# Window attention and PReLU FFN on one core: the turned slice order begins a pair later, y's last sums move behind the division, every second slice's PReLU goes through ScalarE

## The chip, the cores and the metric

The kernel runs on one core of a Trainium2 chip (8 cores). The metric is the device time of one execution in microseconds, the median of several runs.

## What is computed

Windowed attention over 8 batches, 8 heads, 576 positions and head size 64, and behind it a feed-forward layer over the 4608 tokens it gives:

```python
scores = scale * np.matmul(q, k.transpose(0, 1, 3, 2))
mask_plain = (rel >= 0) & (rel < 32)                        # heads 0 to 3
mask_dil = (rel >= 0) & (rel < 128) & (rel % 4 == 0)        # heads 4 to 7
scores = np.where(masks[None], scores, -1000000000.0)
attn = np.exp(scores - np.max(scores, axis=-1, keepdims=True))
attn = attn / (np.sum(attn, axis=-1, keepdims=True) + 1e-09)
x = np.matmul(attn, v).transpose(0, 2, 1, 3).reshape(4608, 512)
h = x @ w_in                                                # 512 to 2048
g = np.maximum(h, 0.0) + alpha * np.minimum(h, 0.0)
out = g @ w_out                                             # 2048 to 512
```

## The kernel before, in words

Each matrix product of the layer is made of three passes over float32r halves: every operand is split into a high half (a cast on ScalarE) and a low half (operand minus high half, on VectorE), and high x high, high x low and low x high are summed in PSUM. Attention is done for 32 pairs of heads, `Pair(b, c)`: `scores` (72 small matmuls), `maxima` (scale and mask from PSUM into `pr`, then the row maxima `nm`, on VectorE), `exponentials` (nine activations on ScalarE, with row sums), `divisions` and `turns` (VectorE: reciprocal, multiplication, transposition into `pt`), `values` (84 small matmuls), and `highs` and `lows`, which bring the result out of PSUM by ScalarE and VectorE.

The layer works on tiles of 512 tokens. Tiles 0 to 2 go slice by slice: a slice (t, f) is one tile and 128 of the 2048 hidden columns. `ffn_h` makes h of a slice (12 matmuls of 128x512 into one PSUM bank), `ffn_relu` and `ffn_sum` (relu(-h) on ScalarE, then one VectorE operation with `bal` = 1 - alpha) or instead `ffn_parts` (two VectorE operations, L490 and L491) apply the PReLU, `ffn_high` and `ffn_low` split g, and `ffn_y` (12 matmuls) adds the slice's share to four banks of y. Tiles 3 to 8 come afterwards, two at a time, in `paired_stage`, which multiplies block sums (Strassen's way) with weights from a ring of ten buffers filled by SP.

Every engine runs its instructions in the order of the program, which is written out by hand. The change lies in the loop `for n in range(CUT, NS)` with CUT = 6 and NS = 48, a step for each slice of the list `slices`: six of tile 0, sixteen of tile 1 (places 6 to 21), ten of tile 0 (22 to 31), sixteen of tile 2. Below, slice n or h(n), y(n), g(n) is the slice at place n of that list. Step n issues h of slice n + 1 and y of slice n - 1. From EARLY = 20 on it also works on a pair: even steps have the scores and maxima of a pair, the pair is divided and transposed two steps later, and its values come in the odd step three later. A step is `turned` when its y comes ahead of h; the other steps have h first. Up to step SECOND - 2 = 20, slices use `ffn_relu` and `ffn_sum`, and weights are still converted; from then on all slices use `ffn_parts`.

The four PSUM banks named "a" serve h, scores and values in turn, the banks "y" the sums of a tile. When a tile's sums are complete (slices 21 and 31, whose `ffn_y` stands in steps 22 and 32, and slice 47 behind the loop), `ffn_y` leaves a function in `ended`, which copies the four banks out and stores them. For tile 0 (slice 31) it adds the part sums that were stored before: `ffn_y` issues their loads into buffers of the tag "m" (five, shared with the PReLU's results), and L526 adds. `split_at` and `combine_at` name odd steps in which GpSimd sums weights for the paired stage (L568, L571) and ScalarE and VectorE split them (L576, L581). `late_ops` holds the token sums of the first paired tiles (`token_parts`: B11, B21, T1 and so on; casts at L666, subtractions at L663 and L669), given to certain steps by `plan_parts`.

Of the kernel before, what the change touches and what calls it, by code (L numbers as in the profile page):

```python
# [37 lines left out]
EARLY = 20  # L38
# [30 lines left out]
def tile_window_attention_prelu_ffn(  # L69
# [404 lines left out]
    def ffn_relu(t, f):  # L474

        ps = ms[t, f]
        m = ffp.tile([P, TT], F32, tag="m", name=f"m_{t}_{f}", bufs=5)
        nc.scalar.activation(out=m, in_=ps, func=AF.Relu, scale=-1.0)
        ms[t, f] = ps, m

    def ffn_sum(t, f):
        ps, m = ms[t, f]
        nc.vector.scalar_tensor_tensor(
            out=m, in0=m, scalar=bal[:, f:f + 1], in1=ps, op0=ALU.mult, op1=ALU.add)
        ms[t, f] = m

    def ffn_parts(t, f):
        ps = ms[t, f]
        m = ffp.tile([P, TT], F32, tag="m", name=f"m_{t}_{f}", bufs=5)
        nc.vector.tensor_scalar(out=m, in0=ps, scalar1=0.0, scalar2=al[:, f:f + 1], op0=ALU.min, op1=ALU.mult)  # L490
        nc.vector.scalar_tensor_tensor(out=m, in0=ps, scalar=0.0, in1=m, op0=ALU.max, op1=ALU.add)  # L491
        ms[t, f] = m

    def ffn_high(t, f):
        g = gbuf([P, 2, TT], F32R, f"g_{t}_{f}")
        nc.scalar.copy(out=g[:, 0, :], in_=ms[t, f])  # L496
        gs[t, f] = g
# [39 lines left out]
    ended = []  # L537
# [56 lines left out]
    for t in range(NSTD, NTILE, 2):  # L594
        for grp in range(NFP // GP):
# [17 lines left out]
            second = [wO[grp, c, j].rearrange("p f a n -> p (f a n)") for c in range(NC) for j in range(GP)]  # L613
# [5 lines left out]
    def slot(n):  # L619
        n %= NRING  # L620
        tag = ("w2_1", "w3_1", "xA1", "xA1", "g0")[n // 2]
        if tag not in ring:
            ring[tag] = (ffp if tag == "g0" else const).tile(
                [P, 8 if tag == "xA1" else 4, 2 * P], F32R, tag=tag, name=f"ring_{tag}",
                **({"bufs": 1} if tag == "g0" else {}))
        t = ring[tag].rearrange("p (s n) w -> p s (n w)", n=2)
        return t[:, n - 4 if tag == "xA1" else n % 2]

    def feed():
        if fed[0] < len(units):  # L630
            to, u = slot(fed[0]).bitcast(F32), units[fed[0]]
            nc.sync.dma_start(out=to if len(u.shape) == 2 else to.rearrange("p (c n) -> p c n", c=2), in_=u)
            fed[0] += 1
# [23 lines left out]
    def token_parts(t):  # L657


        k0, k1, z0, z1 = raw(t, 0), raw(t, 1), raw(t + 1, 0), raw(t + 1, 1)  # L660

        def diff(out, x, y):
            return lambda: nc.vector.tensor_tensor(out=out, in0=x, in1=y, op=ALU.subtract)  # L663

        def high(name, x):
            return lambda: nc.scalar.copy(out=part_of(name, 0), in_=x)  # L666

        def low(name, x):
            return lambda: nc.vector.tensor_tensor(  # L669
                out=part_of(name, 1), in0=x, in1=part_of(name, 0).bitcast(F32), op=ALU.subtract)  # L670

        zeroth = [high("B11", k0), low("B11", k0), high("B21", k1), low("B21", k1)]
        first = [diff(k0, z0, k0), high("T1", k0), low("T1", k0)]
        second = [
            diff(z0, z1, z0), high("T3", z0), diff(k0, z1, k0), high("T2", k0), low("T3", z0),
            diff(k1, k1, k0), low("T2", k0), high("B22", z1), high("T4", k1), low("B22", z1), low("T4", k1),
        ]
        return zeroth, first, second
# [488 lines left out]
    def early_sum(i):  # L1167


        place = []  # L1170

        def load():
            for q, tag in enumerate(("k", "q", "v", "pt")):
                x = att.tile([P, 4 * P], F32, tag=tag, name=f"wy{i}_{tag}").rearrange("p (a c n) -> p a c n", a=2, c=2)
                place.append(x)
                if i:
                    nc.sync.dma_start(out=x[:, 1], in_=wW[i, :, q % 2, q // 2])
                else:
                    high, low = (
                        weight(1, a, q // 2).bitcast(F32)[:, 2 * P * (q % 2):2 * P * (q % 2 + 1)].rearrange(  # L1180
                            "p (c n) -> p c n", c=2) for a in range(2))
                    nc.gpsimd.tensor_tensor(out=x[:, 1], in0=high, in1=low, op=ALU.add)
            combine_out(lambda q: place[q][:, 1])
            for x in place:
                split(x[:, 0], x[:, 1])

        def store():
            for q, x in enumerate(place):
                nc.sync.dma_start(
                    out=wY[i, q % 2, :, q // 2].rearrange("p a c n -> p (a c n)"), in_=x.rearrange("p a c n -> p (a c n)"))  # L1190

        return load, store
# [95 lines left out]
    late_ops = {}  # L1288

    def plan_parts():  # L1290
        zeroth, first, second = token_parts(NSTD)
        late_ops[NS - 9] = zeroth[:2]
        late_ops[NS - 5] = zeroth[2:] + first
        late_ops[NS - 3], late_ops[NS - 2], late_ops[NS - 1] = second[:5], second[5:8], second[8:]


    slices = [(0, f) for f in range(CUT)] + [(1, f) for f in range(NF)] + [(0, f) for f in range(CUT, NF)]
    slices += [(2, f) for f in range(HALF, NF)] + [(2, f) for f in range(HALF)]
    NS = len(slices)
# [127 lines left out]
    for k in range(GP):  # L1427
        first, last = early_sum(k)
# [6 lines left out]
    for n in range(CUT):  # L1435
        scored = pairs[NC + 1 + n] if n + 1 < NC else None
# [58 lines left out]
    score_at, value_at = {}, {}  # L1495
    for p in range(2 * NC, AHEAD):
        n = EARLY + 2 * (p - 2 * NC)
# [5 lines left out]
    for k in range(NFP):  # L1503
        n = SCRATCH + 1 + 2 * k + (2 if k > 1 else 0)
# [2 lines left out]

    for n in range(CUT, NS):
        scored, valued, divided = (at.get(n) for at in (score_at, value_at, divide_at))
        turned = n >= EARLY and n % 2 == 0  # L1510
        if turned:
            ffn_y(*slices[n - 1])
        if n + 1 < NS:
            ffn_h(*slices[n + 1])
        if n <= SECOND - 2:

            ffn_sum(*slices[n])
            ffn_high(*slices[n])
            for w in late:
                w.low()  # L1520
            words = [op for w in now for op in w.words()]
            for op in words[:1]:
                op()
            ffn_low(*slices[n])
            for op in words[1:]:
                op()
            if n + 1 <= SECOND - 2:
                ffn_relu(*slices[n + 1])
            late, now = now, [conversion() for _ in range(quota.pop(0) if quota else 0)]
            ahead()  # L1530
            for op in loads_early.get(n, ()):
                op()
            for w in late:
                w.high()
        elif late:
            late.pop().low()
        while turned and ended:
            ended.pop()()
        if divided:
            divided.divisions()  # L1540
            divided.turns()
        if scored:
            scored.scores()
        if SECOND - 2 <= n < NS - 1:
            ffn_parts(*slices[n + 1])
            ffn_high(*slices[n + 1])
            if not scored:
                ffn_low(*slices[n + 1])
        if not turned:
            ffn_y(*slices[n - 1])  # L1550
        if n in split_at:
            combined_high(split_at[n])
        if valued:
            valued.values()
        if scored:
            scored.maxima()
            ffn_low(*slices[n + 1])
            scored.exponentials()
        if valued:
            valued.highs()  # L1560
            valued.lows()
        while ended:
            ended.pop()()
        if n in split_at:
            combined_low(split_at[n])
        for u in pairs[2 * NC:AHEAD + 1]:
            if u is pairs[2 * NC]:
                due = 2 * (n == SECOND - 4,)
            else:
                due = scored is pairs[pairs.index(u) - 1], valued is pairs[pairs.index(u) - 1]  # L1570
            if due[0]:
                u.load_qk()
            if due[1]:
                u.load_v()
        if SCRATCH <= n < SCRATCH + NF:
            save(n - SCRATCH)
        for op in sums_early.get(n, ()):
            op()
        if n in combine_at:
            combine(combine_at[n], "xB1" if n < SCRATCH + 5 else "xA1")  # L1580
        if n == NS - 9:
            plan_parts()
        for op in late_ops.pop(n, ()):
            op()
        if n >= NS - NRING + 2:
            feed()

    ffn_y(*slices[-1])
    ended.pop()()
    feed()  # L1590
    feed()
    paired_stage()
# [74 lines left out]
```

## Time and profile before

| | |
|---|---|
| median of 3 runs | 853.82 us (852.75 to 858.84) |
| profiled execution | 856.63 us, span 854.8 us |
| TensorE busy | 828.4 us (97%) |
| VectorE, ScalarE, GpSimd busy | 634.6, 448.3, 126.3 us |
| granted TensorE clock, mean | 0.993 |

The span runs from the first to the last instruction; the profiled execution's own time is 1.8 us longer. TensorE's busy time counts matmuls whose ends are modelled, so neighbouring ones overlap by some 0.15 us in the rows: the distance between the starts of two rows tells more than their durations.

### The profile page before, as it was taken

The numbers are of one execution on the slowest core, as the hardware profiler recorded it, in microseconds if no ns is written. First come the engines' busy times: TensorE is split into PE (matmuls) and PEld (weight loads), VectorE is DVE, ScalarE is ACT, GpSimd is POOL, SyncE is SP. The second block draws the span as 40 slices with busy tenths as digits, with TensorE's granted clock in tenths as the row PEclk, the third lists the DMA queues.
The fourth block names the chain that finished last, engine by engine and source line by source line (L and its number), as shares of the span: only waits on it lengthen the run. The fifth ranks groups of instructions, "written<-read, shape, count | busy, mean of one in ns | idle before, by whom it ended". The sixth has DMA issues, their size and how long they took to land.

```text
span 854.8 us, 20630 instructions
## 1 busy us (share of the span) xinstructions
PE 828.4 (97%) x8167; PEld 670.1 (78%) x8167; DVE 634.6 (74%) x1073; ACT 448.3 (52%) x1268; POOL 126.3 (15%) x146
## 2 busy tenths in 40 slices
PE   7889999999989999999999999999999999999997
PEld 5677888788867877778778888788888888888886
DVE  4898888866857787688544988898469878843983
ACT  6786666434324434466534653666366436633650
POOL 0204253510313450030540000000000000000000
PEclk9999999999998999999999999999999999999999
DMA  7765567626897974577887668767766786667663
GB/s 241 257 206 176 188 220 264 204 97 211 269 302 239 304 241 135 180 246 236 260 276 239 194 192 280 249 190 213 223 176 183 219 266 194 195 192 195 193 216 132
DMA packets 123968, 185.71 MB, mean 217 GB/s; under 512 B 10464, under 2 KB 64352, under 8 KB 123872
## 3 DMA queue, kind: packets, MB, share of 16 engines
q1 hardware_dynamic: 123584, 184.13, 69.5%
q8 instruction: 65, 1.06, 0.6%
q14 instruction: 31, 0.25, 0.1%
q10 hardware_dynamic: 288, 0.26, 0.1%
HBM read 138.22 MB, written 46.14 MB: 216 GB/s over the span
## 4 chain that ended last, share of the span: by engine, by line
PE 78%; DVE 11%; DMA 4%; ACT 3%; issue 2%; SPq 1%; ACTq 0%; DVEq 0%
PE pA L684 14%; PE qA L1121 12%; PE h L470 10%; PE y L518 9%; PE pC L684 7%; PE qC L1121 6%; PE y L967 5%; PE pB L684 3%; PE qB L1121 3%; PE o L279 3%; PE s L254 2%; DVE w_dt.float32r L451 2%; DVE wa L440 1%; DMA wW<-wa 1%; DVE g L501 1%
## 5 line engine op out<-in xcount | busy, mean ns | idle before, releaser
L518 PE MATMUL y<-g,w_dt.float32r 128*128 128x512 f32 x576 | 142.4, 396 | 2.1 <-DVE g L501 1.1
L470 PE MATMUL h<-x,w_dt.float32r 128*128 128x512 f32 x576 | 141.0, 393 | 2.0 <-DVE w_dt.float32r L451 1.1
L518 PEld LDWEIGHTS y<-g,w_dt.float32r 128*128 128x128 f32 x576 | 107.9, 190 | 26.2 <-DVE g L501 1.9
L470 PEld LDWEIGHTS h<-x,w_dt.float32r 128*128 128x128 f32 x576 | 106.8, 188 | 25.7 <-DVE w_dt.float32r L451 1.6
L302 ACT ACTIVATE pr<-pr,nm 128x64 f32<-128x64 f32 x216 | 72.1, 336 | 27.2 <-DVE nm L292 27.2
L496 ACT CAST g<-m 128x512 fp32r<-128x512 f32 x48 | 29.6, 616 | 96.2 <-DVE m L491 92.4
L684 PE MATMUL pA<-parts_w,ring_w 128*128 128x512 f32 x234 | 58.4, 391 | 0.0
L684 PE MATMUL pA<-parts_w,ring_xA 128*128 128x512 f32 x228 | 56.4, 390 | 0.0
L837 DVE TENSOR_TENSOR gp<-stage,gp 128x512 fp32r<-128x512 f32 x80 | 53.5, 684 | 3.4 <-ACT gp L833 3.4
L833 ACT CAST gp<-stage 128x512 fp32r<-128x512 f32 x80 | 46.9, 618 | 9.3 <-DVE stage L830 8.1
L684 PEld LDWEIGHTS pA<-parts_w,ring_w 128*128 128x128 f32 x234 | 43.7, 188 | 9.6 <-ACT stage L726 0.5
L684 PEld LDWEIGHTS pA<-parts_w,ring_xA 128*128 128x128 f32 x228 | 42.6, 188 | 9.0 <-ACT stage L947 0.2
L501 DVE TENSOR_TENSOR g<-m,g 128x512 fp32r<-128x512 f32 x48 | 36.7, 764 | 16.6 <-ACT g L496 16.6
L1121 PE MATMUL qA<-gp,ring_xA 128*128 128x512 f32 x192 | 46.4, 390 | 0.0
L1121 PEld LDWEIGHTS qA<-gp,ring_xA 128*128 128x128 f32 x192 | 35.9, 188 | 7.5
L302 ACT ACTIVATION_READ_ACCUMULATOR pr<-pr,nm 128x1 f32 x216 | 40.7, 188 | 0.0
L1121 PE MATMUL qA<-gp,ring_w 128*128 128x512 f32 x168 | 40.5, 389 | 0.0
L1121 PEld LDWEIGHTS qA<-gp,ring_w 128*128 128x128 f32 x168 | 31.5, 188 | 6.5
L289 DVE SCALAR_TENSOR_TENSOR pr<-s,mask_sb 128x320 f32<-128x320 f32 (+1 forms) x48 | 21.6, 450 | 16.9 <-PE s L254 16.9
L811 DVE TENSOR_TENSOR stage<-pC,stage 128x512 f32<-128x512 f32 x25 | 17.2, 688 | 21.7 <-ACT stage L947 21.7
L279 PEld LDWEIGHTS o<-pt,v 32*64 32x64 f32 x1764 | 22.2, 134 | 14.1 <-issue 6.7
L490 DVE TENSOR_SCALAR m<-h,al 128x512 f32<-128x512 f32 x27 | 20.1, 743 | 16.4 <-PE h L470 15.9
(210 smaller groups left out, 1678.1 us busy)
## 6 DMA issues: line engine op xcount, KB each, us to landing
ring_w<-wS SPq DMA_DIRECT2D x68, 256.0 KB, 3.0
ring_xA<-wS SPq DMA_DIRECT2D x67, 256.0 KB, 3.2
v<-vX SPq DMA_DIRECT2D x24, 352.0 KB, 4.3
ring_g<-wS SPq DMA_DIRECT2D x33, 256.0 KB, 3.0
wO<-w_dt.float32r SPq DMA_DIRECT2D x32, 256.0 KB, 4.2
wS<-wc SPq DMA_DIRECT2D x16, 512.0 KB, 4.1
ring_w<-wO SPq DMA_DIRECT2D x32, 256.0 KB, 3.2
ring_xA<-wY SPq DMA_DIRECT2D x32, 256.0 KB, 3.1
```

The costliest lines, as they stand in the source:

```text
L279: nc.tensor.matmul(self.po[c][e * D:(e + 1) * D, a:z, :], lhsT=self.v[rows, (CUT0 + 1) * s + i, :], rhs=self.pt[rows, (r + a) * BK + (BQ i ...
L289: nc.vector.scalar_tensor_tensor(out=self.pr[:, a:z], in0=self.ps[i], scalar=SCALE, in1=mask_sb[:, self.mask + a:self.mask + z], op0=ALU.m ...
L302: nc.scalar.activation(out=self.pr[:, r, :], in_=self.ps[r // CUT0][:, r % CUT0, :] if self.onto else self.pr[:, r, :], func=AF.Exp, bias= ...
L470: nc.tensor.matmul(ms[t, f], lhsT=weight(0, a, f)[:, c * P:(c + 1) * P], rhs=half(t, c)[:, e, :], start=(c == 0 and n == 0), stop=(c == NC ...
L496: nc.scalar.copy(out=g[:, 0, :], in_=ms[t, f])
L501: nc.vector.tensor_tensor(out=g[:, 1, :], in0=ms.pop((t, f)), in1=g[:, 0, :].bitcast(F32), op=ALU.subtract)
L518: nc.tensor.matmul(ys[t][c], lhsT=weight(1, a, f)[:, c * P:(c + 1) * P], rhs=g[:, e, :], start=(first and n == 0), stop=(last and n == 2),)
L684: nc.tensor.matmul(to, lhsT=w[:, (2 * a + c) * P:(2 * a + c + 1) * P], rhs=part_of(name, e)[:, c * TT:(c + 1) * TT], start=start and c == ...
L833: nc.scalar.copy(out=self.pair(n)[:, 0], in_=self.whole(n))
L837: nc.vector.tensor_tensor(out=p[:, 1], in0=self.whole(n), in1=p[:, 0].bitcast(F32), op=ALU.subtract)
L967: nc.tensor.matmul(ys2[tt], lhsT=w[:, k * P:(k + 1) * P], rhs=g[:, e], start=j == 0 and n == 0, stop=j == GF - 1 and n == 2)
L1121: nc.tensor.matmul(named(to)[c], lhsT=w[:, b * P:(b + 1) * P], rhs=rhs[:, e], start=begins and k == 0, stop=i == GP - 1 and k == 2, skip_g ...
```

## The change

Five edits, all of them order or choice of engine; what is computed stays.

1. `turned` holds for even steps from 22 on; step 20 has h first.
2. `ended` in turned steps is emptied behind `divisions`, `turns` and `ffn_parts` (before: ahead of `divisions`). Only steps 22 and 32 have something in it.
3. In odd steps from 21 to 45, the PReLU of the even slice n + 1 (an odd one, counted from 1) goes by `ffn_relu` on ScalarE and `ffn_sum`; even steps keep `ffn_parts`.
4. A pair's `exponentials` move from the end of its even step into the next odd step, between `ffn_relu` and `ffn_sum`.
5. The token sums are given to other steps: `zeroth[2:]` (high and low of B21) from step 43 to 41, `second[9:]` (low of B22 and of T4) from step 47 to behind the last sums of the loop.

```diff
-        late_ops[NS - 9] = zeroth[:2]
-        late_ops[NS - 5] = zeroth[2:] + first
-        late_ops[NS - 3], late_ops[NS - 2], late_ops[NS - 1] = second[:5], second[5:8], second[8:]
+        late_ops[NS - 9], late_ops[NS - 7], late_ops[NS - 5] = zeroth[:2], zeroth[2:], first
+        late_ops[NS - 3], late_ops[NS - 2], late_ops[NS - 1], late_ops[NS] = second[:5], second[5:8], second[8:9], second[9:]
...
-        turned = n >= EARLY and n % 2 == 0
+        turned = n > EARLY and n % 2 == 0
...
-        while turned and ended:
-            ended.pop()()
         if divided:
             divided.divisions()
             divided.turns()
         if scored:
             scored.scores()
         if SECOND - 2 <= n < NS - 1:
-            ffn_parts(*slices[n + 1])
+            if n % 2:
+                ffn_relu(*slices[n + 1])
+                if n - 1 in score_at:
+                    score_at[n - 1].exponentials()
+                ffn_sum(*slices[n + 1])
+            else:
+                ffn_parts(*slices[n + 1])
+            while turned and ended:
+                ended.pop()()
             ffn_high(*slices[n + 1])
...
         if scored:
             scored.maxima()
             ffn_low(*slices[n + 1])
-            scored.exponentials()
...
     ffn_y(*slices[-1])
     ended.pop()()
+    for op in late_ops.pop(NS):
+        op()
```

## Rows read from the trace of the kernel before

**Rows 1.** The page's part 1: busy us, share of the span, instructions.
```profile
PE 828.4 (97%) x8167; PEld 670.1 (78%) x8167; DVE 634.6 (74%) x1073; ACT 448.3 (52%) x1268; POOL 126.3 (15%) x146
```

**Rows 2.** The chain that ended last, 150 to 190 us: start, us, what.
```profile
176.49 2.72 PE h L470 x12
179.20 0.90 PE s L254 x58
...
185.77 1.06 PE o L279 x56
```

**Rows 3.** Timeline of TensorE, 150 to 190 us: start, us, what, idle before.
```profile
157.06 3.49 PE L518 MATMUL y<-g,w_dt.float32r 128*128 128x512 f32 x13
161.69 2.79 PE L518 MATMUL y<-g,w_dt.float32r 128*128 128x512 f32 x11 [1.14 <-DVE g L501]
164.32 2.88 PE L470 MATMUL h<-x,w_dt.float32r 128*128 128x512 f32 x12
```

**Rows 4.** Timeline of VectorE, 148 to 192 us.
```profile
160.95 0.68 DVE L501 TENSOR_TENSOR g<-m,g 128x512 fp32r<-128x512 f32 x1
```

**Rows 5.** Timeline of TensorE, 236 to 300 us.
```profile
249.32 2.88 PE L518 MATMUL y<-g,w_dt.float32r 128*128 128x512 f32 x12
254.51 0.30 PE L279 MATMUL o<-pt,v 32*64 32x32 f32 x4 [2.31 <-DVE pr L289]
...
257.81 1.46 PE L279 MATMUL o<-pt,v 32*64 32x32 f32 x78 [2.14 <-DVE m L491]
...
263.57 2.90 PE L470 MATMUL h<-x,w_dt.float32r 128*128 128x512 f32 x12
...
274.03 3.02 PE L518 MATMUL y<-g,w_dt.float32r 128*128 128x512 f32 x12
...
287.31 3.02 PE L518 MATMUL y<-g,w_dt.float32r 128*128 128x512 f32 x12
```

**Rows 6.** Busy time by windows of 2 us; PEclk is the granted clock.
```profile
260.00:262.00 2.00, 2.00 (x6) 1.52 (x6) 1.93 (x4) 0.00 (x0) 0.94 (x1) 0.50 0.74 242
```

**Rows 7.** Timeline of VectorE, 225 to 266 us.
```profile
247.18 0.69 DVE L526 TENSOR_TENSOR ob<-y,ob 128x512 f32<-128x512 f32 x1 [6.65 <-DMA ob<-part]
248.74 2.03 DVE L526 TENSOR_TENSOR ob<-y,ob 128x512 f32<-128x512 f32 x3 [0.87 <-DMA ob<-part]
...
251.93 0.78 DVE L317 STREAM_TRANSPOSE pt<-pr 128x576 f32<-128x576 f32 x1
...
257.06 0.69 DVE L491 SCALAR_TENSOR_TENSOR m<-h,m 128x512 f32<-128x512 f32 x1
```

**Rows 8.** Timeline of TensorE, 300 to 400 us.
```profile
339.86 1.05 PE L279 MATMUL o<-pt,v 32*64 32x32 f32 x78 [1.27 <-DVE m L491]
...
354.74 0.86 PE L254 MATMUL s<-k,q 64*32 64x64 f32 x64 [0.75 <-DVE ob L528]
```

**Rows 9.** Timeline of VectorE, 305 to 372 us.
```profile
339.12 0.69 DVE L491 SCALAR_TENSOR_TENSOR m<-h,m 128x512 f32<-128x512 f32 x1
...
354.00 1.28 DVE L528 COPY ob<-y 128x512 f32<-128x512 f32 x2
```

**Rows 10.** Timeline of ScalarE, 270 to 306 us.
```profile
273.16 1.05 ACT L576 CAST wc<-wsum_xA 128x1024 fp32r<-128x1024 f32 x1 [0.55 <-PE y L518]
```

**Rows 11.** Groups by line, 163 to 357 us: busy us, mean ns, idle before.
```profile
L302 ACT ACTIVATE pr<-pr,nm 128x64 f32<-128x64 f32 x108 | 36.1, 335 | 4.1 <-DVE nm L292 4.1
L490 DVE TENSOR_SCALAR m<-h,al 128x512 f32<-128x512 f32 x27 | 20.1, 743 | 16.4 <-PE h L470 15.9
...
L669 DVE TENSOR_TENSOR parts_w<-raw_xB,parts_w 128x1024 fp32r<-128x1024 f32 x7 | 8.4, 1221 | 1.1 <-ACT parts_w L666 1.1
L666 ACT CAST parts_w<-raw_xB 128x1024 fp32r<-128x1024 f32 x7 | 7.4, 1058 | 5.0 <-DVE raw_xB L663 4.9
```

**Rows 12.** Line L478, the relu: ns min/median/max, first and last start, forms.
```profile
L478 ACT ACTIVATE m<-h x21: 586/598/681, 39.6 to 159.9; 128x512 f32<-128x512 f32 x21
```

**Rows 13.** Line L311, the multiplication in the division, in the same columns.
```profile
L311 DVE TENSOR_TENSOR pr<-pr,rs x24: 757/760/1678, 177.6 to 636.3; 128x576 f32<-128x576 f32 x24
```

## The prediction

> **What bounds the kernel now.** I read the page first: TensorE is busy 828.4 of 854.8 us [rows 1], so some 26 us of idle time are all that can be won, and only the loop over steps n = 20 to 47 (156 to 356 us) is touched. There I took the idle times out of TensorE's timeline; y(n), h(n) are the products of slice n, counted from 0. In undisturbed steps two slices need 13.28 us, from the start of one y at 274.03 to that two steps on at 287.31 [rows 5], with no idle time noted: they are TensorE's own work, which no shuffling on VectorE or ScalarE shortens. Twelve of its matmuls need 2.72 us, a pair's scores 0.90, its values 1.06 [rows 2]. Four places lose time.
> First, step 20: y(18) begins at 157.06, so h(21), two blocks later, could begin at 157.06 + 2 x 2.72 = 162.50; it begins at 164.32 [rows 3]: 1.8 us lost, because y(19) stands ahead of it and waits for the low half of g(19), written from 160.95 for 0.68 us [rows 4].
> Second, steps 32 to 34: y(32) begins at 249.32 and ends 2.72 later, at 252.04. The values of step 33 (1.06) and y(33) (2.72) should be through at 255.9, but h(35) begins at 263.57 [rows 5]: 7.6 us lost. Some 5 us of it is idle time (2.31 and 2.14 in the rows, and 0.55 between them); the rest is the clock, granted at 0.50 (1.2 GHz) from 260 to 262 after this idle time [rows 6].
> Third, step 45: the values wait 1.27 us for VectorE's L491. Fourth, the first scores of the paired stage wait 0.75 us for a copy of ob [rows 8].
>
> **The change, part by part.**
> *Turned order from n > 20.* At step 20, h(21) and the scores now come ahead of y(19). h(21) begins at 157.06 + 2.72 = 159.8 and ends at 162.5, the scores end at 163.4; g(19) is complete at 161.64 [rows 4]. Nothing waits: the whole 1.8 us is won. Behind h(21) its evacuation is queued on VectorE, which still works on the slice before; it has until y(21), due at 171.6, which covers it. If h(21) itself were to wait for w_in(15), whose low half is converted just before that time, up to 1 us would go back.
>
> *Final sums behind division and parts (steps 22 and 32).* At step 32 VectorE stands 6.65 us at the first of the four adds (L526), waiting for the DMA that brings back the partial sums, and again for the second; the four are through at 250.77 [rows 7]. Only then come division, transposition (from 251.93 for 0.78), parts(33) (0.74 + 0.69), the maxima of the scores (1.7), low(33) (0.68) and parts(34), whose L491 ends at 257.75 [rows 7]. The values of step 33 need the four PSUM banks that h(33), two score tiles and h(34) hold, so they start at 257.81 [rows 5]. In the new order division, transposition and parts(33) run inside the 6.65 us of waiting: h(33) was through before 245.7 (249.32 less 2.72 for h(34) and 0.90 for the scores), so parts(33) end near 247.1, as the first transfer lands. The adds keep their time, to 250.77, since their loads are issued from the same place of SP's queue. Then maxima to 252.5, low(33) to 253.2, and the sum for slice 34 (one operation of 0.7 us in place of two) to 253.9. The values begin at 253.9 in place of 257.81: 3.9 us won. As only 1.8 us stay idle (252.1 to 253.9), little more than the 1.14 at step 20, behind which eleven matmuls took 161.69 to 164.32 [rows 3], which is full speed, I take the slow stretch as gone too: 7.6 - 1.8, less 0.1 for the restart, gives 5.7 us. Bounds: 3.9 if the clock falls all the same, 7.6 if the partial sums land earlier. The stores of the sums stay directly behind their adds, so what SP issues behind them keeps its place; it is needed a step later and lies covered.
> At step 22 two copies of y's banks (0.7 each) move behind parts(23). h(23) is then through at 177.1, 1.9 earlier than now, parts to 178.5, copies to 179.9. y(22) uses the same banks and is due at 180.7: covered by 0.8 us; if that cover fails, TensorE loses what is missing, 0 to 1.4 us.
>
> *Relu on ScalarE in odd steps.* It replaces thirteen VectorE operations of 0.74 us [rows 11] by a relu of 0.60 us [rows 12] on ScalarE, which is busy 52% [rows 1]. The Trainium skill, page ScalarE: Activation LUTs, section Rules for kernel authors, tells authors to put relu, max and min on VectorE and not on ScalarE. This case's rows show the opposite order for a 128x512 f32 tile out of PSUM, 0.60 against 0.74 us, so the measurement decides; by the rule each relu would be the dearer of the two, and the sum would stay as it is, since ScalarE has the time.
> The exponentials move with it: in twelve odd steps they now stand behind the relu and ahead of the slice's high half. Nine of them take 9 x 0.335 = 3.0 us [rows 11]. In time from the start T of an odd step's h: relu 2.9 to 3.5, exponentials to 6.5, high to 7.1. Now the high part of the combined weights begins at 273.16 [rows 10] in step 35, whose T is 274.03 less 2.85 + 2.72 + 1.06, so at T + 5.8; it would begin 1.3 us later. So the values' copies, the weights' low part, division and transposition also come some 1.2 us later and end near T + 12.5. Parts of the next slice can't begin before T + 12.4 anyway, when its h is through. Then maxima, low and the one-operation sum end at T + 17.4; the next values are due at T + 18.95. The delay is hidden by 1.5 us, and nothing is paid in most steps. The multiplication in the division takes 0.76 us alone and up to 1.68 in other places [rows 13], namely beside GpSimd's weight sums; the 12.5 contains 1.6.
>
> *Token sums spread otherwise.* One cast (1.05) and one subtraction (1.22) [rows 11] move from step 43 to 41; low B22 and low T4 (1.22 each) go behind the last copies. Steps 39 and 41 now have such a pair between the delayed weights and the division: there the sum ends at T + 19.1 to T + 19.3 against 18.95. I charge 0.2 and 0.3 us; bounds 0 and 1.2 each. In step 43 VectorE's relief of 1.2 us and the exponentials' delay cancel, but slice 46 needs one operation on VectorE in place of two, so the values of step 45 wait about 0.5 us where they waited 1.27 for an L491 begun at 339.12 [rows 8, 9]: 0.8 us won, bounds 0 and 1.3. At the end the copies of ob no longer stand behind three subtractions, which held them to 354.00 [rows 9]; low T2 alone is ahead, so they end before the scores come: 0.7 won. B22 and T4 are first multiplied six products of 1.36 us on, which covers their low halves.
>
> Sum: 1.8 + 5.7 + 0.8 + 0.7 = 9.0 won, 0.5 paid: 8.5 us. The profiled execution took 856.63 us with its span of 854.8; it would be 848.1. It lies 2.8 us above the median of 853.82. I take the sum off the median, since none of these waits hangs on one execution: 845.3 us, 1.0% less. The paired stage behind is the same work and keeps what is won.
>
> **The rivals.**
> *The values of step 33 wait for another thing.* The relu of slice 34 writes a buffer that the first finished sum leaves, so it waits for that tile's store, issued after 247.9; before, the first operation on that buffer came only after 256. If the store takes over 4.5 us, the relu is late for the sum, and each us more is one lost; with more idle time the clock may fall again. For it: the loads issued for step 32 kept VectorE waiting 6.65 us [rows 7]. Against: the store starts when those loads are through. Cost 2 to 4 us: 847.3 to 849.3.
> *All of it goes.* The partial sums land earlier, and the remaining 1.8 us and the 0.5 each of steps 39, 41 and 45 vanish: 842.5.
> *Slower: the odd steps no longer close.* Relu, exponentials and high on ScalarE and the chain on VectorE up to the next values form a ring around each pair of steps, with a slack of 1.5 us by the rows. If the later division meets more of GpSimd's sums (0.9 us on the multiplication, as much on the small addition ahead of it), every us beyond the slack is paid in each of eleven pairs of steps. From 0.8 us beyond it on, the gain of 8.5 is a loss; 1.6 beyond gives 845 + 18 = 863. For it: steps 39 and 41 already have no slack. Against: the 12.5 above contains the long multiplication. Beside this stands the Trainium skill, page SBUF — State Buffer, section Who interferes with whom: a VectorE instruction with two SBUF inputs and a reading GpSimd contend, and the later one is blocked entirely. The trace agrees in kind (0.76 against 1.68).
> *It does little.* The waits come back a step on, because TensorE arrives earlier at the next late operand: 849.5 to 854.
>
> **How the numbers follow.** Forecast 845.3 us, 843.3 to 847.3: 0.55. Store: 0.17. All gone: 0.10. Little: 0.12. Slower ring: 0.06. From 842 to 850 lies 0.84 of this; the upper end takes in the store rival and the bound of 3.9 for the clock. A measurement of this kernel can tell about 1% from no change, which is 8.5 us, and the forecast stands on this edge: faster by over 1% takes a little over half of the first case and the third, 0.44; within 1% 0.51; slower 0.05.
>
> **What would show it.** Right: in the trace after, h(21) directly behind y(18) with no idle time near step 20; division and transposition before the adds of ob at step 32, one idle time of about 1.8 us ahead of the values of step 33 and a granted clock of 1.00 behind it; a wait of 0.5 us or less at step 45 and none of the first scores of the paired stage; two steps still 13.28 us. Wrong: idle times ahead of the values in many odd steps, h of even steps waiting for banks that the values held, or a clock of 0.50 after step 33.

## The result, and the profile after

The changed kernel takes 846.06 us (median of 4 runs, 843.14 to 847.11) against 855.24 of before beside it: a ratio of 0.9884, 95% interval 0.9837 to 0.9931. Run again later with more runs it gave 847.0 against 855.05 us, 0.991 (0.9891 to 0.9928). So some 8 us are won, 0.9 to 1.2%. The profiled execution's span fell from 854.8 to 845.0 us. The page of after, part 1:

```profile
PE 827.2 (98%) x8167; PEld 668.7 (79%) x8167; DVE 629.0 (74%) x1060; ACT 453.4 (54%) x1281; POOL 128.2 (15%) x146
```

TensorE's own work is the same in count [rows 1]; ScalarE has thirteen instructions more and VectorE thirteen fewer, the relus. What went is nearly all idle time: TensorE's busy time fell by 1.2 of the 9.8 us. TensorE's timeline of after, from step 20 on (start, us, what, idle before and its releaser), answers to [rows 3]:

```profile
155.58 2.88 PE L518 MATMUL y<-g,w_dt.float32r 128*128 128x512 f32 x12
158.87 3.29 PE L470 MATMUL h<-x,w_dt.float32r 128*128 128x512 f32 x12 [0.41 <-ACT w_dt.float32r L448]
162.09 0.97 PE L254 MATMUL s<-k,q 64*32 64x64 f32 x72
162.99 3.06 PE L518 MATMUL y<-g,w_dt.float32r 128*128 128x512 f32 x12
165.89 2.88 PE L470 MATMUL h<-x,w_dt.float32r 128*128 128x512 f32 x12
...
247.28 3.00 PE L518 MATMUL y<-g,w_dt.float32r 128*128 128x512 f32 x12
250.21 0.56 PE L279 MATMUL o<-pt,v 32*64 32x32 f32 x6
252.19 1.17 PE L279 MATMUL o<-pt,v 32*64 32x32 f32 x78 [1.41 <-DVE m L483]
253.28 4.36 PE L518 MATMUL y<-g,w_dt.float32r 128*128 128x512 f32 x12
257.48 2.88 PE L470 MATMUL h<-x,w_dt.float32r 128*128 128x512 f32 x12
...
333.02 1.05 PE L279 MATMUL o<-pt,v 32*64 32x32 f32 x78 [0.35 <-DVE m L483]
334.00 3.02 PE L518 MATMUL y<-g,w_dt.float32r 128*128 128x512 f32 x12
...
345.38 1.52 PE L684 MATMUL pA<-parts_w,ring_w 128*128 128x512 f32 x6
346.83 0.97 PE L254 MATMUL s<-k,q 64*32 64x64 f32 x72
347.73 1.67 PE L684 MATMUL pC<-parts_w,ring_w 128*128 128x512 f32 x6
```

h(21) stands directly behind y(18), with a wait for the weight of that slice (L448); the values of step 33 still wait, and the y behind them takes 4.36 us in place of the 2.9 to 3.0 of other y; the waits of step 45 and of the first scores of the paired stage are 0.35 us and nothing [rows 8]. The windows of after say why y(33) is long: the granted clock (last but two) is at 0.50, 1.2 GHz.

```profile
250.00:252.00 2.00, 0.77 (x8) 0.38 (x6) 1.97 (x5) 1.82 (x11) 0.00 (x0) 1.00 1.13 328
252.00:254.00 2.00, 1.81 (x80) 1.66 (x81) 0.32 (x2) 2.00 (x10) 0.00 (x0) 0.70 0.90 292
254.00:256.00 2.00, 2.00 (x6) 1.53 (x5) 2.00 (x5) 1.07 (x3) 0.00 (x0) 0.50 1.12 354
```

VectorE around step 32 of after shows the new order, and what it still waits for ([rows 7] show before):

```profile
240.55 0.78 DVE L317 STREAM_TRANSPOSE pt<-pr 128x576 f32<-128x576 f32 x1
243.60 0.75 DVE L490 TENSOR_SCALAR m<-h,al 128x512 f32<-128x512 f32 x1 [2.27 <-PE h L470]
244.38 0.69 DVE L491 SCALAR_TENSOR_TENSOR m<-h,m 128x512 f32<-128x512 f32 x1
246.48 2.69 DVE L526 TENSOR_TENSOR ob<-y,ob 128x512 f32<-128x512 f32 x4 [1.41 <-DMA ob<-part]
...
250.79 0.68 DVE L501 TENSOR_TENSOR g<-m,g 128x512 fp32r<-128x512 f32 x1
251.39 0.74 DVE L483 SCALAR_TENSOR_TENSOR m<-m,bal,h 128x512 f32<-128x512 f32 x1
```

Transposition and parts(33) (L490, L491) lie ahead of the adds (L526); the idle time at them fell from 6.65 to 1.41 us. Lengths between marks of TensorE's timeline show where the 9.8 us of the two profiled executions are, and serve for all kernels below (us; each is the difference of two starts, the last one from pC to the end of the span):

| kernel | y(18) to h(22) | y(32) to h(35) | wait at step 45 | pA to pC | pC to end | time, ratio to before |
|---|---|---|---|---|---|---|
| before | 10.97 | 14.25 | 1.27 | 3.31 | 499.3 | |
| after | 10.31 | 10.20 | 0.35 | 2.35 | 497.3 | 846.06, 0.9884 |
| after, again | 10.30 | 10.27 | 0.35 | 2.35 | 497.3 | 847.0, 0.991 |
| turned order alone | 10.05 | 14.24 | 1.27 | 3.31 | 497.5 | 853.8, 0.9981 |
| last sums alone | 13.47 | 10.51 | 1.27 | 3.30 | 497.5 | 849.95, 0.9937 |
| relu and exponentials alone | 10.76 | 13.34 | 1.59 | 3.26 | 497.4 | 856.6, 1.0013 |
| token sums alone | 13.52 | 14.37 | 0.17 | 2.36 | 497.1 | 852.99, 0.9964 |
| order without relu | 9.84 | 10.32 | none | 2.36 | 497.3 | 846.92, 0.9905 |
| loads early | 9.74 | 7.24 | 0.35 | 2.35 | 497.2 | 842.64, 0.9864 |
| loads early, sums between | 10.99 | 7.48 | 0.36 | 2.35 | 497.2 | 845.09, 0.9884 |
| relu, exponentials as before | 10.98 | 13.60 | none | 2.35 | 497.0 | 856.62, 1.0012 |
| order and early loads, no relu | 9.97 | 7.81 | 0.15 | 2.35 | 496.9 | 844.32, 0.9864 |

Two differences of the first two lines are not the change's. The stage ahead of step 20, which no edit touches, ended 1.5 us earlier in the execution of after (y(18) at 155.58 against 157.06), and from pC to the end before took 499.3 us where all eleven others take 496.9 to 497.5: its trace has 1.79 us in which TensorE waits for nothing that the profile shows, and no other trace has them. The row, from before:

```profile
440.94 0.85 PE L967 MATMUL y<-gp,ring_w 128*128 128x512 f32 x3 [1.79 <-issue]
```

### The profile page after: what moved, and what is told of

It reads as the page before. It is cut to its first block, busy times and chain, and to the rows that moved or that the text cites. A ratio compares the mean times of both kernels' runs of the same rounds, so it can differ in the third digit from the quotient of the medians.

```text
span 845.0 us, 20627 instructions
## 1 busy us (share of the span) xinstructions
PE 827.2 (98%) x8167; PEld 668.7 (79%) x8167; DVE 629.0 (74%) x1060; ACT 453.4 (54%) x1281; POOL 128.2 (15%) x146
## 4 chain that ended last, share of the span: by engine, by line
PE 74%; DVE 12%; ACT 6%; DMA 5%; issue 2%; SPq 1%; ACTq 0%; DVEq 0%
PE pA L684 14%; PE qA L1121 12%; PE h L470 8%; PE y L518 7%; PE pC L684 7%; PE qC L1121 6%; PE y L967 5%; PE pB L684 3%; PE qB L1121 3%; PE s L254 2%; PE o L279 2%; DMA ws<-w_in 2%; DVE w_dt.float32r L451 2%; ACT pr L302 2%; DVE wa L440 1%
## 5 line engine op out<-in xcount | busy, mean ns | idle before, releaser
L478 ACT ACTIVATE m<-h 128x512 f32<-128x512 f32 x34 | 20.4, 599 | 27.9 <-PE h L470 22.4
L451 DVE TENSOR_TENSOR w_dt.float32r<-wa,w_dt.float32r 128x512 fp32r<-128x512 f32 x26 | 21.5, 841 | 10.6 <-ACT w_dt.float32r L448 10.4
```

What stands on the lines that cost most here:

```text
L451: nc.vector.tensor_tensor(out=self.dst[1], in0=self.a.bitcast(F32), in1=self.dst[0].bitcast(F32), op=ALU.subtract)
```

## The experiments

**Each edit alone.** Four kernels, each the kernel before with one part of the change.

The turned order:

```diff
-        turned = n >= EARLY and n % 2 == 0
+        turned = n > EARLY and n % 2 == 0
```

> The kernel before with the turned order from step 22 on, nothing else. Theory (each wait of TensorE ends by its own edit): h(21) directly behind y(18), the wait at step 20 gone or shrunk to a short wait for w_in(15); the block up to h(22) 1.5 to 2.1 us shorter, steps 32, 45 and the paired stage as before, in all about 852. Rival (the gain of step 20 only came from an earlier arrival in that one execution): h(22) no earlier, no change.

0.9981 (0.9962 to 1.0), so about 1.6 us, as expected, though the interval reaches down to no change. The block is 10.05 us long. How much it wins depends on the execution: the four traces with the old order there took 10.76 to 13.52 us for this block (12.2 on average), the eight with the turned order 9.74 to 10.99 (10.3). In two of the four, those of the last sums and of the token sums, y(19) waited twice and its matmuls then ran slowly, at a granted clock of about half; in the eight the clock stayed at 1.00 there. From the last sums' kernel, with the window behind the waits:

```profile
155.09 2.88 PE L518 MATMUL y<-g,w_dt.float32r 128*128 128x512 f32 x12
158.91 0.50 PE L518 MATMUL y<-g,w_dt.float32r 128*128 128x512 f32 x1 [0.93 <-ACT g L496]
160.68 4.31 PE L518 MATMUL y<-g,w_dt.float32r 128*128 128x512 f32 x11 [1.27 <-DVE g L501]
```
```profile
162.00:164.00 2.00, 2.00 (x6) 1.52 (x6) 1.26 (x2) 0.53 (x1) 0.00 (x0) 0.51 0.57 195
```

The two turned kernels with 10.98 and 10.99 us show what then comes late: the scores behind h(21) waited 0.90 us for the load of q.

The last sums:

```diff
-        while turned and ended:
-            ended.pop()()
         if divided:
...
             ffn_parts(*slices[n + 1])
+            while turned and ended:
+                ended.pop()()
```

> The kernel before with the last sums behind division, transposition and parts, nothing else. Theory: division, transposition and parts(33) leave the chain behind the adds, two operations for slice 34 stay on it; the values of step 33 begin 3.1 us earlier against y(32), some 5.3 us behind its start; y(33) still at the clock of 0.50; 3 us won in all, about 851. Rival (the relu did it): values as late as before, 8.5 us behind the start of y(32).

0.9937 (0.9913 to 0.996), 5.4 us, more than expected, while its trace shows 3.7 us less for the block at step 32 and the clock again at half. The values begin 5.12 us behind y(32), where 5.3 were expected: the mechanism holds without the relu. That leaves 1.7 us between the median and this block; the interval allows 3.4 to 7.4. The profiled execution, 852.04 us, was itself 2.1 us above the median of 849.95, and the slow y(19) at step 20 made its block there 2.5 us longer than in the trace of before. Whether the other executions were spared that is not shown.

The relu on ScalarE with the late exponentials (edits 3 and 4, as in the diff of the change):

> The kernel before with relu on ScalarE in odd steps and the exponentials behind it, nothing else. Theory: steady pairs of steps stay at 13.3 us; at step 33 one operation of 0.7 less, so 0.7 us won; at step 45 the late exponentials push the token sums and the values wait as long as before or 0.4 longer; in all within 1 us of the kernel before. Rival (ScalarE relieves VectorE everywhere and most of the gain is here): 3 us or more won, waits at step 45 gone.

1.0013 (0.999 to 1.0036): nothing won. The block at step 32 is 0.9 us shorter, but step 45 waits 1.59 us where before waited 1.27, and behind this wait the clock falls (0.61, then 0.53) and y(45) takes 4.59 us. So its trace gives back at step 45 what it won at step 32. TensorE and the windows of this kernel:

```profile
337.43 1.05 PE L279 MATMUL o<-pt,v 32*64 32x32 f32 x78 [1.59 <-DVE m L483]
338.41 4.59 PE L518 MATMUL y<-g,w_dt.float32r 128*128 128x512 f32 x12
```
```profile
336.00:338.00 2.00, 0.57 (x55) 0.57 (x59) 1.35 (x2) 1.08 (x2) 0.00 (x0) 1.00 0.00 0
338.00:340.00 2.00, 2.00 (x48) 1.68 (x38) 1.94 (x7) 0.78 (x7) 0.00 (x0) 0.61 0.28 52
340.00:342.00 2.00, 2.00 (x7) 1.59 (x6) 2.00 (x3) 1.27 (x2) 0.00 (x0) 0.53 0.71 215
```

The token sums:

```diff
-        late_ops[NS - 9] = zeroth[:2]
-        late_ops[NS - 5] = zeroth[2:] + first
-        late_ops[NS - 3], late_ops[NS - 2], late_ops[NS - 1] = second[:5], second[5:8], second[8:]
+        late_ops[NS - 9], late_ops[NS - 7], late_ops[NS - 5] = zeroth[:2], zeroth[2:], first
+        late_ops[NS - 3], late_ops[NS - 2], late_ops[NS - 1], late_ops[NS] = second[:5], second[5:8], second[8:9], second[9:]
```

> The kernel before with the token sums spread as after, nothing else. Theory: the wait of the values at step 45 falls from 1.27 to 0.2 or less, as VectorE gets to that division 1.2 us earlier, and the first scores of the paired stage do not wait; 2 us won, about 852. Rival (step 45 was won by the relu): its wait stays at 1.2, only 0.9 won at the end.

0.9964 (0.994 to 0.9989), 3.1 us; its own marks show 1.1 at step 45 and 0.95 from pA to pC. The wait of step 45 is 0.17 us, less than in the changed kernel: this edit won it, not the relu.

```profile
340.97 1.05 PE L279 MATMUL o<-pt,v 32*64 32x32 f32 x78 [0.17 <-DVE m L491]
```

The four ratios together give 1.6 + 5.4 + 3.1 less 1.1, that is 9.0 us, within the error of the whole.

**The changed kernel again, and without its relu.**

> The changed kernel once more, for a narrower interval and a second trace. Theory (single edits add up: 1.6 + 5.4 + 3.1 less 1.1): 846 to 848, ratio near 0.990; from pC of the paired stage to the end 497.3 us as in all four single edits, so that the 1.8 us wait inside that stage in the trace of before was that execution's alone; clock 0.50 for a stretch behind step 33 again. Rival (the change also shortens the paired stage): 495 us or less from pC to the end.

As expected: its five lengths repeat those of after to 0.1 us, the clock falls behind step 33 again, and pC to the end is 497.3.

The second kernel has the turned order, the last sums and the token sums, with `ffn_parts` for all slices and the exponentials at the end of the even step:

```diff
-            if n % 2:
-                ffn_relu(*slices[n + 1])
-                if n - 1 in score_at:
-                    score_at[n - 1].exponentials()
-                ffn_sum(*slices[n + 1])
-            else:
-                ffn_parts(*slices[n + 1])
+            ffn_parts(*slices[n + 1])
...
             ffn_low(*slices[n + 1])
+            scored.exponentials()
```

> The three edits of order without the relu and the late exponentials: turned order, last sums and token sums as after, odd steps with two VectorE operations and the exponentials where they were. Theory (relu and late exponentials win nothing beside the others): within 1 us of the changed kernel, 845 to 848; values of step 45 wait 0.2, block y(32) to h(35) 10.5. Rival (they need each other): 2 us or more slower than the changed kernel.

846.92 against 847.0 us on the same chip: relu and late exponentials win nothing that can be told beside the other three edits (the intervals are some 2 us either way). Its block at step 32 takes 10.32 us against 10.27.

**What is left of the stall.** SP issues the stores of a weight slice (`save` of step 31) ahead of the loads of the part sums. Here they go behind (`REST` is 31, the place of the slice whose sums end there):

```diff
         if turned:
             ffn_y(*slices[n - 1])
+        if n == REST + 1:
+            save(REST - SCRATCH)
...
-        if SCRATCH <= n < SCRATCH + NF:
+        if SCRATCH <= n < SCRATCH + NF and n != REST:
             save(n - SCRATCH)
```

> The changed kernel, with the stores of one weight slice (step 31) issued behind the loads of the part sums instead of ahead of them. Theory (what is left of the stall at steps 32 to 34 hangs on the landing of these loads, and the low clock on its idle time): the adds begin right behind parts(33), the values of step 33 wait 0.6 or less, y(33) takes 2.9 and the clock stays at 1.00; block y(32) to h(35) 6.9 to 7.2 in place of 10.2, so 3 us faster than the changed kernel, about 843.5. Rival (VectorE's own work sets the time): no earlier.

842.64 us, 0.9864 (0.9841 to 0.9886), the fastest of all kernels here. VectorE adds without waiting, the values wait 0.26 us, and y(33) runs at full clock. VectorE, TensorE and the window behind:

```profile
242.99 2.47 DVE L526 TENSOR_TENSOR ob<-y,ob 128x512 f32<-128x512 f32 x4
```
```profile
248.67 1.05 PE L279 MATMUL o<-pt,v 32*64 32x32 f32 x78 [0.26 <-DVE m L483]
249.65 3.04 PE L518 MATMUL y<-g,w_dt.float32r 128*128 128x512 f32 x12
```
```profile
250.00:252.00 2.00, 2.00 (x10) 1.65 (x9) 0.65 (x2) 2.00 (x8) 0.00 (x0) 1.00 1.11 355
```

The block falls from 10.2 to 7.24 us, 3.0 as expected. The time fell by 4.4 us against the changed kernel in the same rounds; 0.6 more is the shorter block at step 20, where no edit was made, and the rest is within the intervals.

With the loads early, the sums were also put between transposition and parts(33):

```diff
             divided.turns()
+        while turned and ended:
+            ended.pop()()
...
-            while turned and ended:
-                ended.pop()()
             ffn_high(*slices[n + 1])
```

> The kernel with early loads, and the last sums between transposition and parts(33), where VectorE is idle. Theory: the adds run while h(33) is still being multiplied, nothing waits at steps 32 to 34, block 6.5 to 6.7; 3.5 us faster than the changed kernel, about 843. Rival (the loads still land after h(33)): as with parts first, or 1 us worse, since parts(33) then wait behind the adds.

845.09 us, 0.9884 (0.9861 to 0.9907): 1.9 us less than the changed kernel, but the intervals overlap. In its trace the block is 7.48 us, 2.8 shorter than the changed kernel's and not shorter than with parts first (7.24). The expectation failed: the chain of waits has the loads landing 5.21 us after their issue, at 244.43, when h(33) was through as well, so parts(33) did stand behind the adds; and a store took long.

```profile
239.22 5.21 DMA ob<-part
...
244.53 0.70 DVE ob L526
...
245.24 5.07 DMA out<-ob
```

The store of the first sum ran 5.07 us, and the relu of slice 34, which writes that buffer, waited for it. This is the first rival of the prediction, come true in this kernel, but at a price of some 0.2 us: the sum for slice 34 began at 251.03, 0.79 us behind the start of low(33), where after has 0.60 between the two. Here the values wait 0.52 us.

**Do relu and exponentials belong together?** The changed kernel with the exponentials back in the even step, so ahead of the relu on ScalarE:

```diff
                 ffn_relu(*slices[n + 1])
-                if n - 1 in score_at:
-                    score_at[n - 1].exponentials()
                 ffn_sum(*slices[n + 1])
...
             ffn_low(*slices[n + 1])
+            scored.exponentials()
```

> The changed kernel with the relu kept on ScalarE, but the exponentials back at the end of the even step, ahead of that relu. Theory (the two belong together: ScalarE reaches the relu only behind nine exponentials): the relu comes 1.5 to 2.5 us later in every odd step from 21 to 43, the one-operation sum with it, and the values wait 0.2 to 0.8 us in most of eleven pairs of steps, more at step 33; pairs of 13.5 to 14.1 us in place of 13.33; 4 to 10 us slower than the changed kernel. Rival (slack of 1.5 us covers it): as the changed kernel, pairs of 13.33.

856.62 us, 1.0012 (0.9992 to 1.0032): the whole gain is gone, 9 to 10 us, the upper end of what was expected. At step 33 the values wait 3.82 us, at steps 41 and 43 1.21 each (317.06 below). At step 23 they wait 1.33 us, the clock falls behind it, and y(22) takes 4.60 us, so that this pair of steps takes 16.44 us. The others take 13.65 to 14.73 us away from step 33 (scores at 281.62, 295.32, 308.98 and 323.71). ScalarE at step 37 shows the cause: the relu stands behind nine exponentials and begins at 287.23, when its h(38) has been there since 285.3.

```profile
184.29 1.05 PE L279 MATMUL o<-pt,v 32*64 32x32 f32 x78 [1.33 <-DVE m L483]
185.27 4.60 PE L518 MATMUL y<-g,w_dt.float32r 128*128 128x512 f32 x12
...
258.87 1.46 PE L279 MATMUL o<-pt,v 32*64 32x32 f32 x78 [3.82 <-DVE m L483]
...
317.06 1.05 PE L279 MATMUL o<-pt,v 32*64 32x32 f32 x78 [1.21 <-DVE m L483]
```
```profile
186.00:188.00 2.00, 2.00 (x6) 1.56 (x6) 1.90 (x8) 0.08 (x1) 0.00 (x0) 0.51 0.64 176
```
```profile
284.22 0.35 ACT L302 ACTIVATE pr<-pr,nm 128x64 f32<-128x64 f32 x1 [0.36 <-DVE nm L292]
...
287.23 0.57 ACT L478 ACTIVATE m<-h 128x512 f32<-128x512 f32 x1
288.62 0.62 ACT L496 CAST g<-m 128x512 fp32r<-128x512 f32 x1 [0.81 <-DVE m L483]
```

**Early loads without the relu.** The three edits of order with the stores behind the loads (the diffs above).

> The three edits of order with the part sums' loads ahead of the stores, two VectorE operations in odd steps and the exponentials where they were before. Theory (with the loads early the chain behind the adds is what counts, and the relu takes one operation out of it): values of step 33 wait 0.9 where they wait 0.26 with the relu, clock 1.00, block y(32) to h(35) 7.4 to 8; step 45 without a wait; in all within 1 us of the kernel with early loads, about 843. Rival (relu needless): the same block.

844.32 us, 0.9864 (0.9841 to 0.9887), the same ratio as with the relu. The block is 7.81 us against 7.24, since the values wait 0.84 us:

```profile
250.40 1.05 PE L279 MATMUL o<-pt,v 32*64 32x32 f32 x78 [0.84 <-DVE m L491]
251.38 3.03 PE L518 MATMUL y<-g,w_dt.float32r 128*128 128x512 f32 x12
```

So once the loads no longer hide it, the relu takes its 0.6 us out of the chain behind the adds; step 45 gives 0.2 of it back.

## Why the prediction was right, point by point

The forecast of 845.3 us and 8.5 us won stands against 846.06 and 9.2, or 8 in the longer series; the case that came is the first one. One sign that it gave for being wrong, a clock of 0.50 after step 33, came all the same. By its steps:

- *Turned order, 1.8 us.* Alone 1.6 us by its ratio. In the traces of before and after the block is only 0.66 us shorter (10.97 to 10.31); of the 2.1 us by which after reached h(22) earlier, 1.5 were already there at y(18). Over the twelve traces the two orders differ by 1.9 us on average, so the size holds, but not by this pair of traces. "Nothing waits" was too much: three blocks and the scores need 3 x 2.72 + 0.90 = 9.1 us, and the turned kernels took 9.74 to 10.99. The reserve that I named, a wait for w_in(15), came true, in after with 0.41 us ahead of h(21) and a slower h(21) of 3.29; a wait of the scores for the load of q, 0.90 us in two kernels, was not foreseen.
- *Last sums, 5.7 us with bounds of 3.9 and 7.6.* This step was mis-sized: 4.05 us in the trace (14.25 to 10.20). (The loss itself is 7.75 by its own terms, not 7.6: 252.04 + 1.06 + 2.72 is 255.82.) The order worked as worked out: VectorE's division, transposition and parts vanished into the wait, and the values begin 4.9 us behind y(32), where 253.9 - 249.32 = 4.6 were forecast and 8.5 was before. What failed is the sentence that the slow stretch goes too. It rested on 1.14 us of idle time at step 20 that had cost no clock; here the idle time of 1.41 us, with six small matmuls ahead of it, brought the clock to 0.50 again. By an estimate from the windows of both traces it was low for some 3.4 us, where before had some 6.8, part of them idle; but y(33) took 4.36 us, nearly as long as the 4.54 of before (259.19 below). The lower bound was nearly the value. Early loads showed the rest: with 0.26 us of waiting the clock stayed at 1.00 and 3.0 us more came. Perhaps not every execution has the slow stretch: of the ten of the changed kernel, the three with a mean granted clock of 0.999 or more (843.14, 845.28 and 845.62 us) took the least time, the others have 0.993 to 0.998; no trace of those three is there to show it.

```profile
259.19 4.54 PE L518 MATMUL y<-g,w_dt.float32r 128*128 128x512 f32 x12
```

- *Step 22.* y(22) starts at 180.65 without a wait; the cover held.
- *Relu and late exponentials, nothing paid and nothing won but one operation at slices 34 and 46.* Alone they cost 1.1 us by the ratio, in an interval that takes in none, together with the rest nothing (846.92 against 847.0). The 0.7 us at slice 34 was not to be seen beside the last sums, where the values began 5.12 us behind y(32) without the relu and 4.91 with it; the adds ended 0.5 us later against y(32) in the latter. The slack of 1.5 us in the odd steps held: no values of steps 23 to 31 or 35 to 43 waited. That a relu out of PSUM is no slower on ScalarE held too: a median of 0.60 us at L478 and of 0.75 at L490.
- *Steps 39 and 41, 0.5 us paid.* Not paid. But pairs of steps take 13.33 us in place of 13.28, some 0.3 us in all by the marks (0.10 from h(22) to y(32), 0.17 from h(35) to y(44)). The turned order alone and the last sums alone show the same 13.32 to 13.33, the relu alone and the token sums alone 13.29; why is open.
- *Token sums, 0.8 at step 45 and 0.7 at the end.* 0.92 (the wait fell from 1.27 to 0.35) and 0.96 (3.31 to 2.35).

Sum of the marks: 0.66 at step 20, 4.05, 0.92 and 0.96, less 0.27 in the pairs of steps, is 6.3 us; the 1.5 us ahead of y(18) and the 2.0 behind pC, which make up the 9.8 of the two profiled executions, belong to those executions and not to the change. With the 1.9 us that step 20 gives over all traces the sum is 7.6, near the 8 of the longer series. So 8.5 came out close in spite of the 1.65 us missing at step 32: of these, some 0.6 were made up by the 0.5 us that was charged and not fully paid and by the token sums, and the rest lies within the intervals. That is in part luck.

The rival of the store did not come in the changed kernel. ScalarE did wait 3.64 us there for the store of the first sum, issued at 247.20, but the relu of slice 34 was through at 249.96, and VectorE reached its sum only at 251.39, with 1.4 us to spare. ScalarE of after:

```profile
249.36 0.60 ACT L478 ACTIVATE m<-h 128x512 f32<-128x512 f32 x1 [3.64 <-DMA out<-ob]
```

The rival of the ring that does not close did not come with this order either; putting the exponentials ahead of the relu opens the ring, and that costs the whole gain.

## What to carry to other kernels

An engine that stands at a DMA in its written order is free time for whatever comes next in that order: move the work whose operands are there ahead of the waiting instruction, and move the DMA itself ahead of the others on its queue, which was worth another 3.0 us in the trace here, beside 4.05. A wait of TensorE costs more than its length when the clock falls behind it, so the last 1.5 us of such a delay can be worth 3 (the values of step 33 began 4.91 us behind y(32) in after and 3.39 with the loads early, and the block fell by 3.0). When two edits come together, try each alone and each without the other: here the relu on ScalarE won nothing, and without the move of the exponentials it would have cost everything.

## What the runs showed of the hardware that was not expected

The clock fell to about 0.50 behind single waits of 1.33 us (exponentials ahead of the relu, step 23), 1.41 us (after, step 33) and 1.59 us (relu alone, step 45), each with six small matmuls just ahead; behind 1.27 us at the same place of step 45 (before, turned order, last sums) and behind 1.21 us (exponentials ahead of the relu, steps 41 and 43) the y that followed took 3.0 to 3.1 us, its full speed. At step 20 two waits of 0.93 and 1.27 us (last sums) or of 1.10 and 1.09 us (token sums) with one matmul in between were enough, and y(19) took 4.31 and 4.38 us for eleven matmuls, where before, with 1.14 us, it took 2.79 [rows 3].

A relu of 128x512 out of PSUM takes 0.58 to 0.67 us on ScalarE (after, median 0.60); the VectorE operation that it replaced, minimum and multiplication, 0.71 to 0.75 (before, median 0.75). The loads of four times 256 KB landed 5.4 us after their issue behind four stores of weights (after: 241.09 to 246.46) and 5.2 us ahead of them (sums between: 239.22 to 244.43). So a place further forward in the queue did not make them land faster; it helped because they were issued earlier, 9.0 us ahead of y(32) (239.22 against 248.19 with the sums between) in place of 6.2 (241.09 against 247.28 in after).
